# A linear-attention kernel: phi(K) of layer one's first two chunks summed on GpSimd instead of on TensorE

## The chip, the cores and the metric

The kernel runs on one core of one Trainium2 chip. The metric is device time in microseconds for one execution of the whole program. The core has five engines with a queue of instructions each: TensorE (PE, matrix products into PSUM), VectorE (DVE), ScalarE (ACT), GpSimd (POOL), and SyncE (SP, which here only starts DMAs). Each engine executes its queue in order; engines wait for one another through semaphores.

## The reference

The input x has 2048 tokens of 512 features in bfloat16. Two layers are applied, each one linear attention and one MLP, both with a layer norm before and a residual sum behind:

```python
phi = lambda t: where(t > 0, t + 1, exp(t)) + 1e-6
q, k, v = split(layernorm(x) @ wqkv)              # 32 heads of 16 features
pq, pk = phi(q), phi(k)
kv  = einsum("bhsd,bhse->bhde", pk, v)
z   = einsum("bhsd->bhd", pk)                     # sum of phi(K) over all tokens
num = einsum("bhqd,bhde->bhqe", pq, kv)
den = einsum("bhqd,bhd->bhq", pq, z) + 1e-6
x = x + (num / den) @ wo                          # attention half
x = x + gelu(layernorm(layernorm(x)) @ w1 + b1) @ w2 + b2   # MLP half
```

The MLP half norms twice, one norm upon the other. The change concerns `z`: the sum of phi(K) over the tokens, for the first layer.

## The kernel before

**Tiling.** The 2048 tokens are 16 tiles of 128, in four chunks of four tiles. Layer one (in the code layer 0) takes the chunks in the order `C0=(3, 0, 1, 2)`: tiles 12 to 15, 0 to 3, 4 to 7, 8 to 11. Its first stage is, for each tile: statistics of the norm (`stats`, `aggr` on VectorE; `veps`, `pow`, and `nmr` on GpSimd), the normed tile (`norm`, or `cen` and `ysc`), its transpose (`TA` by a DMA from SP's queue, or `PTA` on TensorE and `tcA`, a copy on ScalarE), the product for K (`K`), `exp` and `relu` on ScalarE and `min` and `phik` on VectorE, which leave phi(K) in a buffer of `pkb` (8 buffers), and `G`, four products that add yᵀ·phi(K) in PSUM. The Q products (`Q`) run between them, with `phiq`. At the end of the stage come `cpg` (G copied out), `KV`, `kvm` (a mask), `M`, `cpm`, and then `WO`, the output of the attention, `RA` (residual sum) and the MLP: `statsB` to `normB`, `TB`, `W1` with `gelu`, `W2`, `RB`. `b20` adds the bias b2.

**The sum z.** `attn_z` (line 898) has two ways, chosen by `ZC`, which says for each layer how many of the first chunks are summed the second way.

- For a chunk outside ZC, one operation `Z` is 16 matmuls (lines 937 to 946) of one column each: for each quarter of the features and each of the four tiles, 128x128 of phi(K) is loaded as weights and multiplied with a column of ones. A small VectorE operation (`zs`, line 948 or 951) copies the 128x4 result to `zs`, or adds it.
- For the chunks inside ZC the tiles are added one after another to a float32 accumulator `zacc` (`za`, line 914), on GpSimd unless a table says VectorE. Then VectorE makes a bfloat16 copy (`zhi`, the high half, line 920) and the rest (`zlo`, the low half, line 923), and one operation `ZH` sums both over the partitions with 8 matmuls of one column (lines 930 and 931). `zsh` (line 934) copies the result to `zs`.

```python
if n < cf["ZC"][L]:
    ...
    lambda e, second=second, k=k: e.tensor_tensor(
        zacc[:], pkb[:, zfirst[L].slot, :] if second else zacc[:], pkb[:, pks[k].slot, :], op=ALU.add),
```

Before, `ZC=(0, 3)`: layer one sums all four chunks with `Z0_3`, `Z0_0`, `Z0_1` and `Z0_2`; layer two adds its first three chunks, with seven of the eleven additions on GpSimd.

`zs` is needed at the end of the stage: `zb` (line 1022) makes the matrix with which `D` multiplies phi(Q) for the denominators (line 1085), and `dz` and `ZR` (lines 1027, 1030) make it once more in a row. `ln` and `rec` (lines 1087, 1089) turn D into 1/den on ScalarE, and `pr` multiplies it to phi(Q).

**Order.** The order of the instructions on each engine is written out by hand as lists (`ORDER`, one for each engine). A planner goes through these lists with a table of durations; it only gives out buffers and PSUM banks and then the semaphore waits. In the first stage PSUM leaves four of the eight banks to K, Q, transposes and the small products, since G holds the other four; a K or Q product waits until ScalarE and VectorE have read the bank that it takes. The W products and `WO` use banks 3 to 5.

**Queues.** SP's list holds the loads at the start, the transposes by DMA and the loads of b1 and b2. GpSimd's list holds, between its computations, the loads of `wv`, `wo`, and the halves of `w1` and `w2`; these wait until all transposes of the first stage have landed (`after=trs`, lines 1228 to 1237).

Of the kernel before, what the change touches and what calls it, by code (L numbers as in the profile page):

```python
# [282 lines left out]
def assign_waits(graph, order, sems, dma_sems):  # L283
# [10 lines left out]
    while len(done) < total:  # L294
        moved = False
        for e in ENGINES:
# [45 lines left out]
    C0=(3, 0, 1, 2), N_WARM=8, ZC=(0, 3), LQ='sp', N_HALF=1, N_K=4, N_Q=3, P_Z0=6.15, N_PB=1, N_PT=8, P_DEN=-50.43,  # L342
# [200 lines left out]
def build_kernel(nc, A_x, A_wqkv, A_wo, B_x, B_w1, B_b1, B_w2, B_b2, out, conf=None, report=False):  # L543
# [5 lines left out]
    with ExitStack() as es:  # L549
# [86 lines left out]

        C0 = cf["C0"]
        HC = C0[0]
        FIRST, LAST = 4 * HC, 4 * C0[-1] + 3
        x0 = [Tile(T4, f"x0_{c}") for c in range(NC)]  # L640
# [28 lines left out]
        load_chunk(cf["LQ"], C0[2], -96)  # L669
        load_chunk(cf["LQ"], C0[3], -95)  # L670

# [705 lines left out]
```

## Time and profile before

| what | value |
| --- | --- |
| time, median of 3 runs | 325.48 us (325.1 to 325.51) |
| profiled execution, own time | 325.25 us |
| its span (first to last instruction) | 323.5 us |
| PE busy | 318.4 us (98%) |
| VectorE, ScalarE, GpSimd busy | 216.5, 195.0, 134.8 us |
| granted TensorE clock | 1.000 |

Rows of a timeline give start and duration in us, engine, line, operation, output and input, and a count; in brackets is the idle time of the engine just before and what ended it. A row with x4 is four instructions in a run, and its duration runs from the first start to the last end. Matmuls overlap: in a dense run of 128x512 products one starts about 0.216 us behind the other (four in 0.865 us), though each is recorded with 0.379 us. VectorE's operations overlap a little too: the next begins some 0.08 us before the one ahead has ended. A row of a view by stretches gives, after the length of the stretch, the busy us of PE, PEld (weight loads), VectorE, ScalarE and GpSimd, each with a count, then the granted clock and the DMA's share.

### The profile page before, as it was taken

How to read it: one execution, taken by the hardware profiler on the slowest of the kernel's cores; microseconds unless marked ns; L12 is line 12 of the kernel's file. 1: busy time of each engine (PE TensorE's matmuls, PEld its weight loads, DVE VectorE, ACT ScalarE, POOL GpSimd, SP SyncE). 2: the span in 40 equal slices, each digit the busy share in tenths (PEclk: the TensorE clock that was granted, in tenths of full speed). 3: DMA queues.
4: the chain of work that ended last, by engine and by line, in shares of the span. 5: the costliest groups of instructions: out<-in, count | busy, mean ns of one | idle time of the engine just before them, and what ended most of it. 6: DMA issues, size and time to landing. Idle time of an engine off the chain costs nothing.

```text
span 323.5 us, 4765 instructions
## 1 busy us (share of the span) xinstructions
PE 318.4 (98%) x1698; PEld 159.9 (49%) x1729; DVE 216.5 (67%) x506; ACT 195.0 (60%) x336; POOL 134.8 (42%) x224
## 2 busy tenths in 40 slices
PE   8999999999999999999999999999999999999996
PEld 4444545675444444444444444458644444444443
DVE  4998769999985660213759999999999564000232
ACT  5999698773136129488964657789832644576000
POOL 4673268638703359000266645763541754000000
PEclk9999999999999999999999999999999999999999
DMA  7514558212320206310003200022133133000004
GB/s 239 181 38 91 151 148 290 72 34 56 75 49 9 41 16 99 66 32 2 0 0 68 49 16 2 17 55 47 36 63 82 32 51 81 16 0 2 32 28 152
DMA packets 47028, 20.39 MB, mean 63 GB/s; under 512 B 42076, under 2 KB 45532, under 8 KB 47004
## 3 DMA queue, kind: packets, MB, share of 16 engines
q1 hardware_dynamic: 45532, 15.06, 20.6%
q0 software_dynamic: 1056, 4.72, 4.5%
q10 hardware_dynamic: 416, 0.30, 0.3%
q8 instruction: 14, 0.23, 0.3%
q14 instruction: 10, 0.08, 0.1%
HBM read 8.00 MB, written 2.10 MB: 31 GB/s over the span
## 4 chain that ended last, share of the span: by engine, by line
PE 91%; DVE 7%; issue 1%
PE ps L1180 28%; PE ps L1141 26%; PE ps L860 8%; PE ps L1109 6%; PE ps L878 5%; PE ps L993 4%; PE ps L961 4%; PE ps L891 3%; DVE xsb L1114 2%; DVE stats L742 2%; PE ps L698 2%; DVE yb L782 1%; PE ps L1167 1%; DVE lr L1061 1%; PE ps L1085 1%; DVE rd L1064 1%
## 5 line engine op out<-in xcount | busy, mean ns | idle before, releaser
L1147 ACT ACTIVATE gT<-ps,b1c 128x512 bf16<-128x512 f32 (+1 forms) x140 | 77.0, 600 | 63.3 <-PE ps L1141 62.6
L1141 PE MATMUL ps<-t,w 128*128 128x512 bf16 (+1 forms) x556 | 101.2, 336 | 0.2
L1180 PE MATMUL ps<-w,gT 128*128 128x512 bf16 x424 | 97.6, 379 | 0.5
L1141 PEld LDWEIGHTS ps<-t,w 128*128 128x128 bf16 x560 | 54.7, 98 | 43.8 <-ACT t L815 0.3
L1180 PEld LDWEIGHTS ps<-w,gT 128*128 128x128 bf16 x434 | 42.5, 98 | 50.0
L757 POOL TENSOR_TENSOR rstd<-veps,neghalf 128x1 f32<-128x1 f32 x64 | 38.5, 612 | 5.2 <-DVE veps L755 3.1
L830 ACT ACTIVATE eb<-ps 128x512 bf16<-128x512 f32 x56 | 32.4, 600 | 13.1 <-PE ps L878 6.2
L1190 DVE TENSOR_TENSOR pkb<-ps,xsb 128x512 bf16<-128x512 f32 x15 | 10.1, 684 | 40.7 <-PE ps L1180 40.7
L742 DVE BATCH_NORM_STATS2 stats<-xsb 128x6 f32<-128x512 f32 x48 | 32.2, 677 | 0.3
L860 PE MATMUL ps<-wqkv,t 128*128 128x512 bf16 x125 | 31.1, 379 | 0.2
L1109 PE MATMUL ps<-gtb,t 128*128 128x512 bf16 x123 | 30.1, 379 | 0.3
L841 ACT ACTIVATE rb<-ps 128x512 bf16<-128x512 f32 x38 | 22.2, 601 | 8.9 <-PE ps L860 6.7
L747 POOL TENSOR_SCALAR veps<-mv 128x1 f32<-128x1 f32 x32 | 8.7, 272 | 44.6 <-DVE mv L744 42.2
L755 POOL TENSOR_SCALAR veps<-mv 128x1 f32<-128x1 f32 x28 | 7.2, 262 | 45.1 <-DVE mv L744 43.7
L777 ACT ACTIVATE yb<-xsb,nmr,rstd 128x512 bf16<-128x512 f32 x21 | 16.9, 810 | 11.6 <-POOL nmr L774 11.5
L782 DVE TENSOR_SCALAR yb<-xsb,mv,rstd 128x512 bf16<-128x512 f32 x27 | 14.8, 559 | 11.4 <-POOL rstd L757 11.2
L1186 DVE TENSOR_TENSOR xsb<-ps,xsb 128x512 f32<-128x512 f32 x16 | 10.9, 682 | 16.8 <-PE ps L1180 14.3
L843 DVE TENSOR_SCALAR eb<-eb 128x512 bf16<-128x512 bf16 x46 | 14.5, 329 | 7.8 <-ACT eb L830 7.6
L860 PEld LDWEIGHTS ps<-wqkv,t 128*128 128x128 bf16 x128 | 12.4, 98 | 14.6 <-ACT eb L830 0.3
L878 PE MATMUL ps<-wqkv,t 128*128 128x512 bf16 x76 | 19.4, 379 | 0.2
L1109 PEld LDWEIGHTS ps<-gtb,t 128*128 128x128 bf16 x128 | 12.4, 98 | 14.2 <-ACT gtb L974 0.5
L1126 POOL TENSOR_TENSOR xsb<-xsb,b2b 128x512 f32<-128x512 f32 x14 | 17.3, 1235 | 1.0 <-DVE yb L782 0.7
(103 smaller groups left out, 395.9 us busy)
## 6 DMA issues: line engine op xcount, KB each, us to landing
w<-in_B_w_dram POOLq DMA_DIRECT2D x4, 896.0 KB, 7.8
out_dram<-pkb SPq DMA_DIRECT2D x15, 128.0 KB, 2.0
t<-in_A_x_dram SPq DMA_DIRECT2D x3, 512.0 KB, 7.0
t<-yb SPq DMA_TRANSPOSE x56, 2.5
wqkv<-in_A_wqkv_dram SPq DMA_DIRECT2D x1, 512.0 KB, 5.4
wqkv<-in_A_wqkv_dram POOLq DMA_DIRECT2D x1, 512.0 KB, 4.4
wo<-in_A_wo_dram POOLq DMA_DIRECT2D x1, 512.0 KB, 5.1
t<-t SPq DMA_TRANSPOSE x20, 2.4
```

What stands on the lines that cost most here:

```text
L742: G.op("dve", lambda e: e.bn_stats(stats[:, s.slot, :], src()), 602, reads=src_keys, writes=[k + "s"], tiles=[s, *src_tiles], prio=prio, n ...
L757: G.op("pool", lambda e: e.tensor_tensor(rstd[:, s.slot:s.slot + 1], veps[:, s.slot:s.slot + 1], neghalf[:], op=ALU.pow), 530, reads=[k + ...
L782: G.op("dve", lambda e: e.tensor_scalar(yb[:, y.slot, :], src(), stats[:, s.slot, 2:3] if by_act else mv[:, s.slot, 0:1], rstd[:, s.slot:s ...
L830: G.op("act", lambda e: e.activation(eb[:, et.slot, :], bank(bt), ACT.Exp, scale=factor()), 569 if by else 483, reads=[src_key, *more], wr ...
L841: G.op("act", lambda e: e.activation(rb[:, rt.slot, :], bank(bt), ACT.Relu, scale=factor()), 569 if by else 478, reads=[src_key, *more], w ...
L860: ins = e.matmul(bank(b), lhsT=yTa(yT)[:, dt, k * P:(k + 1) * P], rhs=wqkv[:, dt, D:2 * D], start=(dt == 0), stop=(dt == DT - 1))
L878: ins = e.matmul(bank(b), lhsT=yTa(yT)[:, dt, k * P:(k + 1) * P], rhs=wqkv[:, dt, 0:D], start=(dt == 0), stop=(dt == DT - 1))
L1109: ins = e.matmul(bank(wb), lhsT=yTa(pq)[:, kt, k * P:(k + 1) * P], rhs=gtb[:, kt, :], start=(kt == 0), stop=(kt == DT - 1))
L1126: G.op("pool" if on_pool else "dve", lambda e: e.tensor_tensor(xsb[:, st, :], xsb[:, st, :], b2b[:], op=ALU.add), 1120 if on_pool else 600 ...
L1141: ins = e.matmul(bank(b, n), lhsT=w1[:, dt, ft * P:(ft + 1) * P], rhs=yTa(yT)[:, dt, k0 * P:k1 * P], start=(dt == 0), stop=(dt == DT - 1))
L1147: G.op("act", lambda e, ft=ft, b=b, k0=k0, k1=k1, n=n: e.activation(gT[:, g.slot, ft * 512 + k0 * P:ft * 512 + k1 * P], bank(b, n), ACT.Ge ...
L1180: ins = e.matmul(bank(b), lhsT=gT[:, g.slot, ft * 512 + k * P:ft * 512 + (k + 1) * P], rhs=w2[:, ft, :], start=(ft == 0), stop=(ft == FT - 1))
```

## The change

`ZC` goes from `(0, 3)` to `(2, 3)`. In layer one the chunks 3 and 0 are now summed the second way:

- `Z0_3` and `Z0_0` (16 matmuls each) and VectorE's `zs0_3` and `zs0_0` are gone.
- GpSimd has seven new additions of 128x512: `za0_13`, `za0_14`, `za0_15`, `za0_0`, `za0_1`, `za0_2`, `za0_3`.
- VectorE has `zhi0`, `zlo0` and `zsh0`; TensorE has `ZH0` with 8 matmuls. `Z0_1` and `Z0_2` stay, and are added to `zs`.

With it the lists of all five engines are new in the first stage, up to the first products of the MLP; from `W10_0_13_1` on TensorE's list is as before. No other operation is added, removed or given to another engine. The lines of the file behind the lists move down by one.

```diff
-    C0=(3, 0, 1, 2), N_WARM=8, ZC=(0, 3), LQ='sp', ...
+    C0=(3, 0, 1, 2), N_WARM=8, ZC=(2, 3), LQ='sp', ...
 pe:
-  "warm PTA0_12 idle0_0 PTA0_13 K0_12 idle0_1 K0_13 PTA0_14 Q0_3_0 Q0_3_2 PTA0_15 G0_12_0 K0_14 K0_15 "
-  "Q0_3_3 Q0_3_1 G0_13_0 PTA0_1 G0_14_0 K0_0 Z0_3 G0_15_0 K0_1 K0_3 K0_2 Q0_0_2 Q0_0_3 G0_0_0 G0_1_0 Q0_0_0 "
-  "K0_8 G0_2_0 G0_3_0 K0_5 Z0_0 K0_4 K0_6 K0_7 Q0_0_1 K0_10 K0_11 Q0_1_0 K0_9 Q0_1_3 Z0_1 G0_4_0 Z0_2 "
-  ...
-  "WO0_0_0 WO0_0_1 WO0_0_2 WO0_0_3 D0_1_3 WO0_1_0 WO0_3_0 WO0_2_0 Q0_2_3 WO0_5_0 WO0_4_0 WO0_6_0 PTB0_0 "
-  "WO0_7_0 W10_0_12_0 ..."
+  "warm PTA0_12 idle0_0 PTA0_13 K0_12 idle0_1 K0_13 PTA0_14 Q0_3_0 K0_14 PTA0_15 G0_12_0 Q0_3_3 K0_15 "
+  "PTA0_1 Q0_3_1 G0_13_0 K0_1 Q0_3_2 K0_0 G0_14_0 K0_3 G0_15_0 G0_0_0 Q0_0_3 Q0_0_2 K0_2 G0_1_0 K0_5 Q0_0_0 "
+  "G0_2_0 K0_4 K0_6 G0_3_0 K0_10 K0_8 G0_4_0 Q0_0_1 K0_7 G0_5_0 K0_11 K0_9 Q0_1_1 ZH0 Q0_1_3 Z0_1 Z0_2 "
+  ...
+  "WO0_0_0 WO0_0_1 WO0_0_2 WO0_0_3 D0_1_3 WO0_1_0 WO0_2_0 WO0_3_0 Q0_2_3 WO0_7_0 WO0_5_0 WO0_6_0 PTB0_0 "
+  "WO0_4_0 W10_0_4_0 ..."
 act:
-  "... expk0_13 reluq0_3_0 reluk0_13 tcA0_15 ..."
+  "... expk0_13 reluk0_13 expq0_3_0 tcA0_15 ..."
 dve:
-  "... mink0_14 yscA0_13 statsA0_10 normA0_1 yscA0_14 phik0_14 ..."
-  "... aggrA0_5 aggrA0_10 minq0_3_2 statsA0_8 zs0_3 phiq0_3_2 ... mink0_5 mink0_4 zs0_0 phik0_5 phik0_4 ..."
-  "... minq0_2_0 kvm0_2 kvm0_1 kvm0_0 kvm0_3 phiq0_2_0 cpm0_2 ..."
+  "... mink0_14 statsA0_8 statsA0_5 statsA0_7 normA0_2 ... mink0_0 aggrA0_7 phik0_0 statsA0_4 statsA0_6 ..."
+  "... statsA0_9 mink0_2 phik0_2 aggrA0_9 statsA0_11 aggrA0_11 phik0_3 ... phik0_7 zhi0 zlo0 mink0_11 phik0_11 mink0_9 zsh0 ..."
+  "... kvm0_0 kvm0_2 minq0_2_0 kvm0_1 kvm0_3 phiq0_2_0 cpm0_2 ..."
 pool:
-  "... vepsA0_2 powA0_2 vepsA0_5 powA0_5 nmrA0_5 vepsA0_8 powA0_8 vepsA0_10 ... powA0_11 nmrA0_9 phik0_6 w1_1 "
-  "phiq0_1_2 wv wo w2_1 phiq0_1_1 w1_0 pr0_0_2 pr0_1_0 pr0_1_1 w2_0 pr0_1_2 pr0_1_3 vepsB0_1 powB0_1 vepsB0_0 "
-  "powB0_0 b20_0 vepsB0_2 powB0_2 vepsB0_3 powB0_3 phiq0_2_3 pz0_2_1 ..."
+  "... vepsA0_2 powA0_2 za0_13 vepsA0_5 powA0_5 nmrA0_5 vepsA0_8 powA0_8 za0_14 ... powA0_10 nmrA0_6 za0_15 nmrA0_10 "
+  "powA0_7 za0_0 nmrA0_7 ... powA0_9 nmrA0_9 za0_1 za0_2 phik0_6 za0_3 wv w1_1 wo phiq0_1_2 w2_1 phiq0_1_1 pr0_1_0 "
+  "pr0_0_2 pr0_1_1 w1_0 w2_0 pr0_1_2 pr0_1_3 vepsB0_1 ... powB0_3 phiq0_2_3 b20_0 pz0_2_1 ..."
 sp:
-  "... TA0_11 TA0_9 b1 b2 Tb1 TB0_1 TB0_2 TB0_3 TP0_2_0 TB0_5 TB0_7 ..."
+  "... TA0_11 b1 TA0_9 Tb1 TB0_1 TB0_2 TB0_3 TP0_2_0 b2 TB0_5 TB0_7 ..."
```

More of the change, by code (lines that the diff above doesn't have):

```diff
@@ L341 @@
     LAND={'x0': 3220, 'x1': 4450, 'wk1': 5200, 'wk0': 6080, 'x2': 6750, 'wq': 8250, 'xc0': 9520, 'xc1': 10800, 'xc2': 12050},
-    C0=(3, 0, 1, 2), N_WARM=8, ZC=(0, 3), LQ='sp', N_HALF=1, N_K=4, N_Q=3, P_Z0=6.15, N_PB=1, N_PT=8, P_DEN=-50.43,
+    C0=(3, 0, 1, 2), N_WARM=8, ZC=(2, 3), LQ='sp', N_HALF=1, N_K=4, N_Q=3, P_Z0=6.15, N_PB=1, N_PT=8, P_DEN=-50.43,
     P_A2=-55.11, P_W1=38.59, P_W2=10.23, P_K=55.79, P_G=131.85, P_Q=170.13, STEP=3.86, A1_Q=12.91, A1_STEP=0.5, N_H=4,
```

107 rows, old and new, of the table ORDER are left out of this document.

## The prediction

> **What bounds the kernel now.** I read the page's first part, then busy time by stretches, then the waits of TensorE.
>
> ```profile
> span 323.5 us, 4765 instructions
> PE 318.4 (98%) x1698; PEld 159.9 (49%) x1729; DVE 216.5 (67%) x506; ACT 195.0 (60%) x336; POOL 134.8 (42%) x224
> ...
> PEclk9999999999999999999999999999999999999999
> ```
> ```profile
> 20.00:40.00 20.00, 19.89 (x134) 9.64 (x135) 16.25 (x50) 16.95 (x33) 8.87 (x20) 1.00 0.41 99
> 40.00:60.00 20.00, 19.89 (x105) 9.61 (x106) 17.02 (x37) 17.43 (x32) 14.35 (x17) 1.00 0.63 202
> 60.00:80.00 20.00, 19.84 (x148) 14.22 (x149) 19.96 (x49) 13.30 (x30) 11.76 (x18) 1.00 0.21 44
> 280.00:300.00 20.00, 19.95 (x92) 9.05 (x93) 0.91 (x2) 13.56 (x22) 0.00 (x0) 1.00 0.00 1
> ```
> ```profile
> PE ps L698 <- PEq L1362: 0.8, 1, 0.8
> ```
>
> TensorE is busy 19.84 to 19.95 of every 20 us, at the full clock, and its only listed wait is the start of the program. So it bounds the kernel from its first products to its last, and two things follow. Whatever leaves TensorE's queue is saved in full, and nothing beyond that can be saved. And every wait that a new order puts before a TensorE instruction is lost in full, because no gap stands behind it to take it up.
>
> **What TensorE loses.** Two groups of 16 one-column matmuls go, and one of 8 comes.
>
> ```profile
> 37.27 0.54 PE L942 MATMUL ps<-onesm,pkb 128*128 128x1 bf16 x16
> 37.67 1.02 PE L961 MATMUL ps<-pkb,yb 128*128 128x512 bf16 x4
> ```
>
> The group that stays in the same form, Z0_1, starts at 37.27 and the next operation at 37.67: 0.40 us for 16, 25 ns each. So 2 x 16 - 8 = 24 matmuls are 0.60 us. That is the gain, and also its ceiling: 0.18% of the time.
>
> The Trainium skill ("TensorE: Matmul & The Clock Gate", Back-to-back issue gap) gives about 81 ns for each pair of weight load and matmul in a sustained stream at 128 columns, because the weight load counts too; 24 such pairs would by that be worth an estimated 1.94 us. The two rows, with weight loads in them, show 25 ns, so I keep 0.60 and give the rule a small chance below.
>
> **What VectorE and GpSimd get.** The same operations stand in layer two.
>
> ```profile
> L914 POOL TENSOR_TENSOR zacc<-zacc,pkb x6: 1152/1248/1534, 166.0 to 187.1; 128x512 f32<-128x512 f32 x6
> L914 POOL TENSOR_TENSOR zacc<-pkb x1: 1157/1157/1157, 164.1 to 164.1; 128x512 f32<-128x512 bf16 x1
> L920 DVE TENSOR_SCALAR dz<-zacc x1: 414/414/414, 188.4 to 188.4; 128x512 bf16<-128x512 f32 x1
> L923 DVE TENSOR_TENSOR eb<-zacc,dz x1: 679/679/679, 188.9 to 188.9; 128x512 bf16<-128x512 f32 x1
> ```
> ```profile
> 10.00:18.00 8.00, 7.95 (x57) 4.02 (x57) 7.92 (x28) 8.00 (x15) 4.57 (x13) 1.00 0.38 103
> 18.00:26.00 8.00, 7.91 (x37) 3.56 (x37) 7.80 (x25) 7.56 (x15) 7.22 (x18) 1.00 0.18 38
> 26.00:34.00 8.00, 7.95 (x52) 3.81 (x51) 5.74 (x19) 7.84 (x15) 1.18 (x3) 1.00 0.48 97
> 34.00:42.00 8.00, 7.89 (x65) 4.07 (x66) 6.71 (x20) 5.55 (x11) 2.21 (x2) 1.00 0.42 134
> ```
>
> GpSimd gets 1.16 + 6 x 1.25 = 8.7 us. From 10 to 26 us it is busy 4.57 and 7.22 of 8, from 26 to 42 only 1.18 and 2.21. The list puts three additions in the first 16 us and four in the second, so there is room, though the norms' `pow` and `nmr` queue behind each addition and the transposes of later tiles wait for them. VectorE gets 0.41 + 0.68 us and one small copy, and loses two. It takes them after `phik0_7`, near 36 us, where 8.00 - 6.71 = 1.29 us of the stretch are idle. All of this is off TensorE's path as long as VectorE's phi and norm arrive in time, so in itself I cost it at nothing. The cover is VectorE's idle time: 0.28 us from 10 to 26, but 2.26 + 1.29 = 3.55 us from 26 to 42.
>
> **The additions hold VectorE.** This is the cost that the trace of before shows only in layer two.
>
> ```profile
> 176.91 1.15 POOL L914 TENSOR_TENSOR zacc<-zacc,pkb 128x512 f32<-128x512 f32 x1
> ```
> ```profile
> 177.74 0.48 DVE L843 TENSOR_SCALAR eb<-eb 128x512 bf16<-128x512 bf16 x1 [0.69 <-ACT eb L830]
> ```
> ```profile
> L843 DVE TENSOR_SCALAR eb<-eb x46: 230/288/877, 8.5 to 237.2; 128x512 bf16<-128x512 bf16 x46
> ```
>
> An addition runs from 176.91 to 178.06. The `min` that VectorE starts at 177.74 takes 0.48 instead of the median 0.29: it got going near the end of the addition. So one addition holds a fast VectorE operation for anything from 0 (VectorE is in statistics or in a read of PSUM) to its whole 1.15 us. The new list runs `za0_13` beside three statistics and `za0_14` beside `phik0_0`, which reads PSUM, and two statistics: near 0. The other five lie beside `min`, `phik` and `norm`. I take half a length, about 0.6 us, for each: the order on both engines is fixed, but where in an addition the fast operation falls is not. That is 5 x 0.6 = 3.0 us, less than the 3.55 us of idle time. What remains for TensorE are places where a bank or a phi(K) comes late: `phik0_2` before G0_2, right behind `za0_15`, where TensorE is due as it ends, and `phik0_4`, which frees the bank of K0_8. I take 0.20 us for both. The ends: 0, and 5 x 1.15 - 3.55 = 2.20 us.
>
> The Trainium skill says the same more sharply ("SBUF — State Buffer", Who interferes with whom): the port pair of VectorE and GpSimd is an exclusive lock, and whoever is second fully blocks. The 0.48 agrees with a block until shortly before the end; the rule speaks against this change and stands behind the second rival.
>
> **A new wait at the head.** Before, G0_12 and K0_14 lay between the transpose PTA0_15 and K0_15, the first product that needs tile 15 (`tcA0_15`). Now K0_14 runs ahead of PTA0_15, and Q0_3_3, which needs tile 15, follows G0_12 at once.
>
> ```profile
> 8.58 0.60 ACT L815 ACTIVATE t<-ps 128x512 bf16<-128x512 bf16 x1
> ...
> 10.77 0.63 ACT L815 ACTIVATE t<-ps 128x512 bf16<-128x512 bf16 x1
> ```
> ```profile
> 9.22 0.11 PEld L878 LDWEIGHTS ps<-wqkv,t 128*128 128x128 bf16 x2 [0.33 <-ACT t L815]
> ```
> ```profile
> 11.19 0.38 PE L860 MATMUL ps<-wqkv,t 128*128 128x512 bf16 x1
> ```
>
> The copy at 8.58 (`tcA0_14`) let a weight load go at 9.22, 0.64 us later. ScalarE has the same number and kinds of operations ahead of `tcA0_15` as before, so that still starts at 10.77 and releases at 11.41; TensorE is free for it at 11.19 (where K0_14 started). Cost 0.22 us, bounds 0.15 to 0.30 by what ScalarE's operations scatter. In the old order K0_14 covered it.
>
> **The end of the stage.** `minq0_2_0` ran in a wait for TensorE; now it stands between the four masks `kvm`.
>
> ```profile
> 49.79 0.28 DVE L834 TENSOR_SCALAR eb<-eb 128x512 bf16<-128x512 bf16 x1
> 50.39 0.88 DVE L1035 TENSOR_TENSOR kvb<-ps,bdmask 128x128 bf16<-128x128 f32 x4 [0.32 <-PE ps L1016]
> ...
> 57.88 0.54 DVE L782 TENSOR_SCALAR yb<-xsb,mv,rstd 128x512 bf16<-128x512 f32 x1
> ```
> ```profile
> 58.45 6.67 SPq L792 DMA_TRANSPOSE t<-yb  x3
> ```
> ```profile
> 61.00 8.48 PE L1141 MATMUL ps<-t,w 128*128 128x256 bf16 x76
> ```
>
> From 50.39 VectorE runs without a gap to `normB0_1` at 57.88; its transpose leaves at 58.45, and the first W1 product, at 61.00, needs it. So VectorE is nearly as late as TensorE here, and 0.2 us more before it is 0 to 0.2 us for TensorE: I take 0.10.
>
> **Steps moved past queues.** GpSimd now starts `w1_0` after `pr0_1_1` instead of ahead of the three `pr`, and SP starts `b2` behind TP0_2_0.
>
> ```profile
> 50.04 2.40 POOL L1093 TENSOR_TENSOR t<-t,lr 128x512 bf16<-128x512 bf16 x2 [0.45 <-ACT lr L1089]
> ```
> ```profile
> w<-in_B_w_dram POOLq DMA_DIRECT2D x4, 896.0 KB, 7.8
> ```
> ```profile
> 66.28 1.19 SPq L1077 DMA_TRANSPOSE t<-t  x1
> ```
> ```profile
> b2b<-in_B_b_dram SPq DMA_DIRECT2D x1, 128.0 KB, 3.1
> ```
> ```profile
> t<-yb SPq DMA_TRANSPOSE x56, 2.5
> ```
> ```profile
> 69.44 1.15 POOL L1061 TENSOR_TENSOR lr<-t,zrow 128x512 f32<-128x512 bf16 x1 [1.75 <-DVE t L847]
> ```
> ```profile
> 72.24 0.65 DVE L1064 TENSOR_REDUCE rd<-lr 128x32 f32<-128x512 f32 x1
> ```
> ```profile
> 79.35 1.26 SPq L792 DMA_TRANSPOSE t<-yb  x1
> ```
> ```profile
> 82.75 1.46 PE L1141 MATMUL ps<-t,w 128*128 128x256 bf16 x8
> ```
>
> `w1_0` leaves at about 52.4 and lands 7.8 us later, at 60.2, against a need at 61.00: hidden by 0.8. `wv` and `wo` leave earlier than before and are no danger. `b2` leaves at 66.28 + 1.19 = 67.5 and lands at about 70.6. `b20_0` waits for it, and behind it on GpSimd `pz0_2_1` (69.44 before) goes to about 71.8 and ends at 73.0. VectorE's `red0_2_1` at 72.24 needs it and comes about 0.8 us late, with all that is behind, down to `normB0_4`, whose transpose left at 79.35. A transpose lands 2.5 us later, so near 82.7 instead of 81.9. The first product of the next chunk is the fifth of the row at 82.75; four of the smaller ones ahead of it take 4 x 8.48 / 76 = 0.45, so it is due at 83.2. Hidden by 0.5: nothing. `b1` now goes ahead of TA0_9, which is wanted by the last K product of the stage, and `b20_0` itself is wanted only by the residual sum behind W2: nothing. A buffer of phi(K) is now held until its addition is done; the last one, tile 3's, is taken by `phik0_9`, the last phi(K) in VectorE's list: nothing.
>
> **The sum.** -0.60 + 0.22 + 0.20 + 0.10 = -0.08 us. Made against the profiled execution's 325.25 us it is 325.2; the median of the runs stands 0.23 higher, at 325.48, so 325.4. About 0.2% (0.65 us) is what a measurement of this kernel can tell from no change.
>
> **The rivals.**
>
> *All of the gain stays* (chance 0.13): ScalarE reaches `tcA0_15` earlier and the additions fall beside statistics. 325.48 - 0.60 = 324.9. For it: TensorE had no wait in the old order, which was as tight. Against it: the head's wait hangs on ScalarE, which is busy 8.00 of 8.
>
> *The additions push VectorE behind TensorE* (0.24): slower. Place: from `za0_15` to `za0_3`. The price is 5w - 3.55 us for an average hold w. With the 0.28 of gain that the head and the end leave (0.60 - 0.32), the kernel is slower by over 0.65 once 5w - 3.55 exceeds 0.93, so from w = 0.90 on; at w = 1.15 it is 2.20 - 0.28 = 1.9 us slower, 327.4. I would expect some 326.4 in this case. For it: VectorE's lists are mostly fast operations there. Against it: 0.19 us was the hold in the row above.
>
> *A moved load comes late* (0.15): `w1_0` at W1's start, or `b2` through `red0_2_1` and TB0_4. For it: four steps hang on `b2` in a stretch where VectorE is busy 19.96 of 20. Against it: both are hidden by the medians. It decides when `w1_0` takes over 61.00 - 52.4 = 8.6 us, or when TB0_4 lands after 83.2; 1.2 us more than reckoned on the second path costs 1.2 - 0.5 = 0.7, so about 326.1.
>
> *Weight loads count too* (0.02): the one-column matmuls cost 81 ns where they stand between big ones; then 325.48 - 1.94 + 0.52 = 324.1.
>
> **How the numbers follow.** My forecast, the gain taken back by small waits, has 0.46, with its own range of 325.0 to 325.9. Faster by over 0.65 us can come from the last rival and from a part of the first, whose 0.60 lies just short of it and whose runs scatter by 0.41 us (325.1 to 325.51): 0.02 + 0.05 = 0.07. Slower: 0.22 of the second rival, 0.10 of the third, 0.05 of the forecast's tail: 0.37. Same is the rest, 0.56. The range goes from 324.8, just under the whole gain, to 326.9, inside the second rival, of which the dearer third stays out.
>
> **What would show it.** In the new profile Z's line should have 48 matmuls instead of 80 and line 931 twice four; TensorE should show a wait of about 0.2 us near 11.2 on ScalarE's copy. Between 24 and 36 us `min` and `phik` on VectorE should be recorded up to a microsecond longer beside an addition. If TensorE's rows between 26 and 38 us run on without a gap, the second rival is wrong; if W1's first product starts at 60.5 or before, the end of the stage costs nothing; if `b20_0` starts by 68 or VectorE has no wait near 72, the move of `b2` was free. The prediction is wrong if a wait of a microsecond or more shows on TensorE anywhere, or if its waits add up to less than 0.2 us.

## The result, and the profile after

Over nine executions of each kernel the change took the time from 325.17 to 326.96 us (medians): a ratio of 1.0051, with a 95% interval of 1.004 to 1.0061. So the kernel became slower by about 1.7 us, 0.5%. The forecast was 325.4, with a range up to 326.9; the time lies just above the range, on the side that had a chance of 0.37. The profiled execution of the changed kernel took 327.28 us, with a span of 325.5, against 325.25 and 323.5 before. Behind the lists every line number is one higher than before.

The page's first part, the waits of TensorE, and the stretches:

```profile
span 325.5 us, 4758 instructions
PE 320.0 (98%) x1705; PEld 157.8 (48%) x1705; DVE 220.8 (68%) x507; ACT 195.1 (60%) x336; POOL 144.1 (44%) x231
```
```profile
PE ps L1142 <- issue: 0.9, 1, 0.9
PE ps L699 <- PEq L1363: 0.8, 1, 0.8
PE ps L962 <- DVE pkb L837: 0.5, 1, 0.5
PE ps L1142 <- DMA t<-yb: 0.3, 1, 0.3
```
```profile
26.00:34.00 8.00, 7.54 (x36) 3.18 (x34) 7.66 (x19) 7.30 (x14) 7.00 (x13) 1.00 0.36 74
60.00:80.00 20.00, 19.05 (x145) 13.81 (x144) 18.63 (x45) 12.66 (x29) 11.30 (x17) 1.00 0.26 46
```

Where one wait stood, at the start of the program, there are now four. Two of the new ones show in the stretches: from 26 to 34 us TensorE is busy 7.54 us instead of 7.95, and from 60 to 80 us 19.05 instead of 19.84. (The counts of matmuls can't be compared: some records are missing in each trace.) The two places, in the timeline:

```profile
25.45 1.03 PE L892 MATMUL ps<-t,wqkv 128*128 128x512 bf16 x4
26.94 1.04 PE L962 MATMUL ps<-pkb,yb 128*128 128x512 bf16 x4 [0.46 <-DVE pkb L837]
```
```profile
60.47 1.04 PE L1110 MATMUL ps<-gtb,t 128*128 128x512 bf16 x4
62.45 8.46 PE L1142 MATMUL ps<-t,w 128*128 128x256 bf16 x76 [0.95 <-issue]
```

The first is G0_2. The four products ahead of it take 0.865 us, so it was due at 26.32 and is 0.62 late. The second is the first W1 product: it starts 1.98 us behind the start of the last WO group, where it was 61.00 - 60.13 = 0.87 before.

To see all of the difference I cut the span at six instructions of TensorE: the first Q product (Q0_3_0), the first M product (the end of the first stage), the last WO group, the first W1 product, the WO products of the last chunk, and the matmul ZR of layer two. Each number is the difference of the starts of two rows; the runs below the first three are those of the next section.

```
kernel       start..Q0_3_0  ..M    ..last WO  ..W1   ..WO, last chunk  ..ZR    ..end   span
before           8.36      42.69    9.08      0.87      29.52         105.06   127.9   323.5
after            8.15      43.18    9.14      1.98      29.49         105.21   128.4   325.5
s1 (after)       8.56      42.91    9.13      2.24      29.49         105.20   128.0   325.5
e2               8.37      42.69    9.08      1.81      29.49         105.06   127.9   324.4
s2               8.63      43.18    9.14      0.87      29.64         105.12   128.3   324.9
s4               8.49      43.24    9.14      0.87      29.54         105.29   127.9   324.5
s3               8.78      42.70    9.08      0.88      29.55         105.06   128.0   324.0
e3               8.43      42.60    9.12      1.37      29.49         105.15   128.0   324.2
r12              8.81      42.61    9.13      0.88      29.55         105.21   127.9   324.1
r9               8.17      43.79    9.13      2.08      29.49         105.06   127.9   325.6
```

The start scatters between 8.15 and 8.81 from execution to execution in kernels of either kind; the wait of 0.3 at 246 us (the column before the span) also comes and goes. The rest is the change's: +0.2 to +0.5 in the first stage, although 0.60 us of matmuls left it; +1.1 and +1.4 at the first W1 product; and +0.15 between the last chunk's WO and ZR, over 100 us behind the last instruction that was moved.

### The profile page after: what moved, and what is told of

Same layout as the page of the kernel before. It is cut to its first block, busy times and chain, and to the rows that moved or that the text cites. A ratio compares the mean times of both kernels' runs of the same rounds, so it can differ in the third digit from the quotient of the medians.

```text
span 325.5 us, 4758 instructions
## 1 busy us (share of the span) xinstructions
PE 320.0 (98%) x1705; PEld 157.8 (48%) x1705; DVE 220.8 (68%) x507; ACT 195.1 (60%) x336; POOL 144.1 (44%) x231
## 4 chain that ended last, share of the span: by engine, by line
PE 87%; DVE 7%; ACT 2%; DMA 2%; issue 1%; POOL 1%; ACTq 0%
PE ps L1142 29%; PE ps L1181 25%; PE ps L1110 8%; PE ps L861 7%; PE ps L994 4%; PE ps L879 4%; PE ps L962 3%; PE ps L892 2%; DVE stats L743 1%; DMA t<-yb 1%; ACT eb L831 1%; PE ps L1168 1%; DVE xsb L1115 1%; PE ps L1086 1%; DMA t<-in_A_x_dram 1%
## 5 line engine op out<-in xcount | busy, mean ns | idle before, releaser
L758 POOL TENSOR_TENSOR rstd<-veps,neghalf 128x1 f32<-128x1 f32 x64 | 39.3, 626 | 4.9 <-DVE veps L756 3.0
L861 PE MATMUL ps<-wqkv,t 128*128 128x512 bf16 x128 | 32.0, 379 | 0.2
L1110 PE MATMUL ps<-gtb,t 128*128 128x512 bf16 x128 | 30.9, 379 | 0.0
L844 DVE TENSOR_SCALAR eb<-eb 128x512 bf16<-128x512 bf16 x46 | 15.3, 344 | 7.8 <-ACT eb L831 7.7
L879 PE MATMUL ps<-wqkv,t 128*128 128x512 bf16 x80 | 20.4, 379 | 0.1
```

The source lines that it names most:

```text
L758: G.op("pool", lambda e: e.tensor_tensor(rstd[:, s.slot:s.slot + 1], veps[:, s.slot:s.slot + 1], neghalf[:], op=ALU.pow), 530, reads=[k + ...
L861: ins = e.matmul(bank(b), lhsT=yTa(yT)[:, dt, k * P:(k + 1) * P], rhs=wqkv[:, dt, D:2 * D], start=(dt == 0), stop=(dt == DT - 1))
L879: ins = e.matmul(bank(b), lhsT=yTa(yT)[:, dt, k * P:(k + 1) * P], rhs=wqkv[:, dt, 0:D], start=(dt == 0), stop=(dt == DT - 1))
L1110: ins = e.matmul(bank(wb), lhsT=yTa(pq)[:, kt, k * P:(k + 1) * P], rhs=gtb[:, kt, :], start=(kt == 0), stop=(kt == DT - 1))
```

## The experiments

The theory after the first look was that the first W1 product waits because w1_0, which now leaves GpSimd right ahead of w2_0, holds up the transpose TB0_1 that W1 needs; and that the rest is VectorE, held by the additions. The rivals were that the late VectorE behind the moved b2 and b20_0 is what costs, and that the new order costs by itself. Where an expectation names a theory by a letter, A is the load of w1, B the additions as the whole loss, C the late b2, D the load of w1 and the late b2 side by side, of which TensorE pays the larger, and E that the late b2 costs nothing.

### The load of w1

**e2**: the kernel before, with only w1_0 moved.

```diff
 pool (before):
-  "... w2_1 phiq0_1_1 w1_0 pr0_0_2 pr0_1_0 pr0_1_1 w2_0 ..."
+  "... w2_1 phiq0_1_1 pr0_0_2 pr0_1_0 pr0_1_1 w1_0 w2_0 ..."
```

> The kernel before, without any addition, with the one step moved the other way: w1_0 behind pr0_1_1, directly ahead of w2_0 (52.4 instead of 47.66). Theory A: TB0_1 lands 3.5 us or more after its issue at 58.45, the first W1 product goes from 61.00 to about 62.1, and the kernel takes 326.3 us instead of 325.2. Theories B and C: 325.2, within 0.2, since neither the additions nor b2 are in it.

Measured: 1.0035 (1.0024 to 1.0046), about 1.1 us. The table has all of it in one column, 1.81 instead of 0.87. In e2's timeline:

```profile
61.95 8.46 PE L1141 MATMUL ps<-t,w 128*128 128x256 bf16 x76 [0.78 <-issue]
```

Why, is seen in what the DMA engines do around TB0_1. After, both halves leave in one run (the row below); before, w1_0 left at 47.66 and w2_0 at 52.38, behind three `pr`.

```profile
52.80 1.73 POOL L683 DMA_DIRECT2D w<-in_B_w_dram  x2
```

The first half, w1_0, is in time: it lands 4.9 us after its issue, at 57.7. But w2_0, right behind it, lands at 61.8, where before it landed at 60.3. TB0_1 leaves SP's queue at 58.45 before, at 58.79 after and at 58.46 in e2, where the stretches of one microsecond from 58 on read, before and after (the last two columns are the DMA engines' share and GB/s):

```profile
58.00:59.00 1.00, 1.00 (x6) 0.45 (x5) 1.00 (x3) 1.00 (x4) 0.75 (x2) 1.00 0.07 29
```
```profile
58.00:59.00 1.00, 1.00 (x6) 0.49 (x5) 1.00 (x3) 1.00 (x3) 0.83 (x3) 1.00 1.01 393
```

And the time from issue to landing of that one transpose, before, after, and in e2:

```profile
DMA to landing us min/median/max: 2.4/2.4/2.4
```
```profile
DMA to landing us min/median/max: 3.6/3.6/3.6
```
```profile
DMA to landing us min/median/max: 3.4/3.4/3.4
```

With w2_0 still in flight the transpose takes 1.0 to 1.2 us longer. Full DMA engines at its issue are not enough for that: in e5, a run shown further down, TB0_1 leaves at 59.30, from 59 to 60 the share is 1.05 at 365 GB/s, and it still lands after 2.4 us. Its own data, 544 small packets, start to move only about 1.2 us after the issue, when most of the load is through. These are the DMA views of 2 us from there, after (from 60.0), in e5 (from 60.4) and in e2 (from 59.2): packets, MB, and the time that they took as a share of 16 engines. Queue q1 carries the transpose, q0 the load, q8 instructions.

```profile
q1 hardware_dynamic: 535, 0.13, 71.2%
q0 software_dynamic: 12, 0.04, 5.3%
```
```profile
q1 hardware_dynamic: 544, 0.13, 32.8%
q0 software_dynamic: 4, 0.00, 0.7%
```
```profile
q1 hardware_dynamic: 544, 0.13, 69.7%
q0 software_dynamic: 20, 0.02, 4.1%
q8 instruction: 1, 0.02, 3.4%
```

Undisturbed, the packets of the transpose take 32 to 33% (before, e4, e5). After, 12 packets of the load are left when they begin, and come one or two at a time until 61.3; 44 packets of the transpose follow only from 61.2 on. In e2 the load is through when they begin, at 59.6, but one packet with instructions, which started at 59.2, takes 1.1 us of an engine. The same holds in the other slow traces: s1 and e3 have packets of the load left, r9 has an instruction packet. So TB0_1 seems to be late because a single DMA engine is late. That it is one engine is not shown outright, since the views don't name the engine of a packet; it is read from the packets that come singly.

**s1**: the changed kernel once more, unaltered, for the scatter of this wait.

> The changed kernel as it is, once more, as the base line for the other runs of this group and for a second trace of W1's start. 1.6 us above the kernel before. If the wait at W1's start is the rule with w1_0 in its new place, it is there again, 0.8 us or more; if it comes and goes, it may be 0 to 1.0.

Measured: 1.0042 (1.0028 to 1.0055). The wait is there again, 1.20 us, the landing 3.8 us. Over all runs with w1_0 directly ahead of w2_0 (after, s1, e2, r9, e3, e4, e5) TB0_1 landed after 3.6, 3.8, 3.4, 3.7, 3.0, 2.4 and 2.4 us: the wait comes in five of seven traces. In the eleven traces with w1_0 earlier (before, e1, e6, e7, e8, r10, r11, r12, s2, s3, s4) it was 2.4 or 2.5 each time, without a wait. In e4 and e5 the loads are as close together, but the load's last packets of 4 KB are through when the transpose's begin, at 60.2 and 60.5; w2_0 lands 7.0 us after its issue there, against 7.6 to 8.5 in the five slow traces. Why the end of the load varies so from execution to execution stays open.

**e1**: w1_0 ahead of the `pr`, about where it was before. **s2**: w1_0 much earlier, right behind `wo`.

```diff
 pool (after), e1:
-  "... phiq0_1_1 pr0_1_0 pr0_0_2 pr0_1_1 w1_0 w2_0 ..."
+  "... phiq0_1_1 w1_0 pr0_1_0 pr0_0_2 pr0_1_1 w2_0 ..."
 pool (after), s2:
-  "... wo phiq0_1_2 ... pr0_1_1 w1_0 w2_0 ..."
+  "... wo w1_0 phiq0_1_2 ... pr0_1_1 w2_0 ..."
```

> The changed kernel with one step moved: GpSimd starts w1_0 right behind phiq0_1_1 again, ahead of pr0_1_0, pr0_0_2 and pr0_1_1 (about 48.6 us instead of 52.80). Theory A (the late load: w1_0 and w2_0 leave together at 52.80, still occupy the DMA engines when the transpose TB0_1 leaves at 58.79, and W1's first product waits for it): TB0_1 lands 2.4 to 2.6 us after its issue instead of 3.6, the first W1 product starts near 61.4 instead of 62.45, and the kernel takes about 325.9 us, 1.1 less than the 326.96 of the changed kernel. Theory B (the additions hold VectorE, and the whole loss comes from there): 327.0, within 0.2. Theory C (b2 comes late for b20_0 and VectorE's red0_2_1): 327.0, within 0.2.

> The changed kernel with w1_0 right behind wo on GpSimd (near 38.7 us, where GpSimd has nothing to do, so that no pr is pushed back), buffers and PSUM banks as in the changed kernel, b2 and b20_0 left late. Theory A alone (the late w1_0 costs W1's start about a microsecond, b2's move costs TensorE nothing in these banks): 0.9 us below the changed kernel, 0.7 to 0.8 above the kernel before. Theory D (TensorE pays the larger of the two, so b2's part is still paid): no gain against the changed kernel.

Measured: e1 1.0052 (1.004 to 1.0064), no gain at all; s2 1.0032 (1.0019 to 1.0045). In both the wait at W1 is gone, TB0_1 lands after 2.5 us. In e1 part of what was gained there is lost again elsewhere, 0.42 us between M and the last WO (9.56 against 9.14): issuing the load keeps GpSimd for 0.76 us, the products of den behind it move back by that much, and now one of them lies beside VectorE's `minq0_2_0`, between the masks for M, which takes 0.72 us instead of 0.28:

```profile
51.57 0.72 DVE L835 TENSOR_SCALAR eb<-eb 128x512 bf16<-128x512 bf16 x1
```

Behind `wo` nothing of VectorE's is in the way, and the table has 0.87 for s2 in that column, as before the change. The profiled span of s2 is 0.6 us shorter than that of after and s1: less than the column's 1.1 and 1.4. Against after, s2 loses 0.15 behind W1 and began 0.48 later; against s1 it also has the wait at 246 us and a longer stage. Between the ratios lie 0.3 to 0.6 us; if the wait doesn't come in every execution, the ratios hold only a part of it.

### The load of b2 and its addition

**e4**, **e5**: in the changed kernel, b2 back to its old place, and in e5 b20_0 too. **e8**: in the kernel before, both moved to their new places.

```diff
 sp (after), e4 and e5:
-  "... b1 TA0_9 Tb1 TB0_1 TB0_2 TB0_3 TP0_2_0 b2 TB0_5 ..."
+  "... b1 TA0_9 b2 Tb1 TB0_1 TB0_2 TB0_3 TP0_2_0 TB0_5 ..."
 pool (after), e5 also:
-  "... powB0_0 vepsB0_2 ... phiq0_2_3 b20_0 pz0_2_1 ..."
+  "... powB0_0 b20_0 vepsB0_2 ... phiq0_2_3 pz0_2_1 ..."
 sp and pool (before), e8: the same two moves the other way
```

> The changed kernel with one step of SP moved: b2 ahead of Tb1 (near 34 us) instead of behind TP0_2_0 (67.98). Theories A and B: 327.0 us, within 0.2, b20_0 starting some 2 us earlier and no TensorE row before 80 us moving. Theory C: red0_2_1 and what is behind it on VectorE come earlier, and the kernel gains 0.4 us or more: 326.5 or less.

> Theory D: two late steps lie side by side, each good for about a microsecond, and TensorE pays the larger: W1's start through the transposes behind w1_0 and w2_0 (1.0 in the profile of the changed kernel, none in that of the last experiment), and near 76 us the bank that RB0_1 on VectorE frees, behind b2, b20_0 and pz0_2_1. Here b2 goes ahead of Tb1 and b20_0 behind powB0_0 as in the kernel before, and w1_0 stays late. D: RB0_1 comes about 1.3 us earlier, no TensorE wait near 76, but W1's start may still wait, by 0 to 1.0 us from one execution to the next: 0.4 to 1.4 us above the kernel before, and a wide scatter. Theory E (the move of b2 and b20_0 does nothing, since VectorE is late for other reasons, the additions' lock): 1.6 us above the kernel before, as the changed kernel.

> The kernel before, without any addition, with b2 behind TP0_2_0 on SP and b20_0 behind phiq0_2_3 on GpSimd as in the changed kernel. Theory D: pz0_2_1 and with it red0_2_1 on VectorE come about 1.3 us late, RB0_1 too, and TensorE waits near 76 us for its bank: 0.8 to 1.3 us above the kernel before. Theory E and the prediction's own reckoning (hidden by 0.5): within 0.2 of the kernel before.

Measured: e4 1.0054 (1.0042 to 1.0066), e5 1.0031 (1.0019 to 1.0042), e8 1.0037 (1.0025 to 1.005). By e8 the move of b2 would cost 1.2 us. But e4 and e8 each have a wait of about a microsecond on PSUM that neither kernel has, in e8:

```profile
90.72 1.04 PE L1141 MATMUL ps<-t,w 128*128 128x512 bf16 x4 [0.96 <-DVE xsb L1186]
```

The planner hands out the PSUM banks by going through the lists, and with b20_0 elsewhere it gave this W1 product the bank of another residual sum, one that is read later. So both runs have two changes in one, and show nothing of the load. In e5 the banks are those of the changed kernel; but that profile was one of the two without a wait at W1, so it too has two causes.

**s3**: as e8, with the two steps moved behind the planner's work, so that every bank stays as before. **s4**: e5 with w1_0 as in s2.

```diff
 s3, behind the planner:
     order = sch.run()
+    for q, n, to in (("pool", "b20_0", "pz0_2_1"), ("sp", "b2", "TB0_5")):
+        o = order[q].pop([o.name for o in order[q]].index(n))
+        order[q].insert([o.name for o in order[q]].index(to), o)
```

> The kernel before with b2 behind TP0_2_0 and b20_0 ahead of pz0_2_1, moved after the planner has given out buffers and banks, so that these are all as in the kernel before (in the earlier run with this move the planner gave W10_1_0_0 the bank that RB0_2 frees, not RB0_3). Theory A alone, and the prediction's reckoning: VectorE is about 1.2 us late from red0_2_1 on, but TensorE does not wait for it: within 0.2 of the kernel before. Theory D: 0.8 us or more above it, as in the earlier run.

> The changed kernel with w1_0 right behind wo and b2 and b20_0 at their old places, banks as in the changed kernel. Theory A alone: the same as with w1_0 behind wo only, 0.7 to 0.8 us above the kernel before. Theory D: the only one of this group that gains against the changed kernel, by 0.9.

Measured: s3 0.9999 (0.999 to 1.0008); s4 1.0024 (1.0015 to 1.0033). In s3 the steps are late: GpSimd stands still for 3.09 us until b2 has landed, and `red0_2_1` on VectorE starts at 73.90 instead of 72.24, of which 0.44 is the later start of this execution (W1 at 61.44 against 61.00). TensorE has no wait for it (29.55 from W1 to the last chunk, against 29.52):

```profile
71.15 1.15 POOL L1126 TENSOR_TENSOR xsb<-xsb,b2b 128x512 f32<-128x512 f32 x1 [3.09 <-DMA b2b<-in_B_b_dram]
```
```profile
73.90 0.69 DVE L1064 TENSOR_REDUCE rd<-lr 128x32 f32<-128x512 f32 x1 [0.22 <-POOL lr L1061]
```

So the late b2 costs nothing; that rival falls, and what e8 seemed to show was the bank. s4 is the fastest of the variants with whole additions, and is still 0.8 us slower than the kernel before.

### The additions

**e3**: the additions of layer one, from the second on, on 32 of the 512 columns, so that z leaves those tiles out in the other columns. **r12**: the same, with b2 and b20_0 as in e5 and w1_0 as in s2.

```diff
-    lambda e, second=second, k=k: e.tensor_tensor(
-        zacc[:], pkb[:, zfirst[L].slot, :] if second else zacc[:], pkb[:, pks[k].slot, :], op=ALU.add),
+    lambda e, second=second, k=k, w=D if second or L else 32: e.tensor_tensor(
+        zacc[:, 0:w], pkb[:, zfirst[L].slot, 0:w] if second else zacc[:, 0:w], pkb[:, pks[k].slot, 0:w], op=ALU.add),
```

> The changed kernel with its additions on GpSimd cut to 32 of the 512 columns from the second addition of layer one on (the sum z of the first two chunks leaves these tiles out in the other columns), all lists as they are: each of the six takes about 0.1 to 0.2 us instead of 1.15. Theory A: only the waits of the stage of K and G go, above all the 0.46 us ahead of G0_2, so about 326.3 us, and W1's first product still waits about a microsecond. Theory B: the loss goes as a whole, 325.2 us or, with the 0.60 us of TensorE's work that is saved, down to 324.6. Theory C: 327.0.

> Everything undone but the new order of the first stage and TensorE's smaller work: b2 and b20_0 at their old places, w1_0 right behind wo, and the additions of layer one from the second on cut to 32 of 512 columns (the sum z leaves these tiles out in the other columns). If the loss is the sum that the traces give so far (the moved queue steps, 0.58 us of lock ahead of G0_2, 0.2 us near 186 us), the stage of K and G takes about 42.6 us from Q0_3_0 to M, no TensorE wait is listed besides the start, and the kernel takes 0.0 to 0.3 us more than the kernel before. If something is not accounted for: 0.6 us or more above it.

Measured: e3 1.0019 (1.0009 to 1.0029), r12 1.0006 (0.9997 to 1.0016). In the changed kernel the `min` ahead of G0_2's phi(K) runs beside `za0_15` (VectorE, then GpSimd, then VectorE again):

```profile
25.36 0.79 DVE L835 TENSOR_SCALAR eb<-eb 128x512 bf16<-128x512 bf16 x1
26.19 0.69 DVE L837 SCALAR_TENSOR_TENSOR pkb<-ps,eb 128x512 bf16<-128x512 f32 x1
```
```profile
24.85 1.15 POOL L915 TENSOR_TENSOR zacc<-zacc,pkb 128x512 f32<-128x512 f32 x1
```

With the narrow additions of r12 it takes 0.28, and G0_2 starts with no wait in brackets, 0.96 behind the start of the operation ahead (26.11), so 0.10 late instead of 0.62:

```profile
26.01 0.28 DVE L835 TENSOR_SCALAR eb<-eb 128x512 bf16<-128x512 bf16 x1
```
```profile
24.93 0.25 POOL L915 TENSOR_TENSOR zacc<-zacc,pkb 128x32 f32<-128x32 f32 x1
```
```profile
27.07 1.04 PE L962 MATMUL ps<-pkb,yb 128*128 128x512 bf16 x4
```

The stage falls from 43.18 to 42.60 and 42.61 us: the additions' hold on VectorE costs TensorE 0.58 us there, some 0.53 of it at this place. (In s1, where G0_2 is 0.54 late, the stage takes 42.91, and the hold is worth 0.3.) But without any hold the stage is only 0.09 us shorter than before, though 0.60 us of matmuls are gone. So the new lists cost about 0.5 us by themselves. In r12 all of it shows as gaps between dense runs: 0.27 ahead of Q0_3_3, 0.13 ahead of K0_0, the 0.10 at G0_2 and 0.03 ahead of K0_3. The first is the wait for `tcA0_15` that the prediction names for the head. PTA0_15 starts at 10.54; its four products take 0.22 and the four of G0_12 0.865, so Q0_3_3 was due at 11.62:

```profile
10.54 0.39 PE L806 MATMUL ps<-idp,yb 128*128 128x128 bf16 x4
11.89 1.04 PE L879 MATMUL ps<-wqkv,t 128*128 128x512 bf16 x4
```
```profile
11.89 0.55 PEld L879 LDWEIGHTS ps<-wqkv,t 128*128 128x128 bf16 x4 [0.59 <-ACT t L816]
```

**r11**: the hold moved instead of removed. Loads as in r12, additions whole, and `za0_15` one norm step later, with the banks kept.

```diff
 r11, behind the planner:
     order = sch.run()
+    names = [o.name for o in order["pool"]]
+    za = order["pool"].pop(names.index("za0_15"))
+    order["pool"].insert([o.name for o in order["pool"]].index("za0_0"), za)
+    nm = order["pool"].pop([o.name for o in order["pool"]].index("nmrA0_7"))
+    order["pool"].insert([o.name for o in order["pool"]].index("za0_15"), nm)
```

> The changed kernel with b2 and b20_0 at their old places, w1_0 right behind wo on GpSimd (near 38.7 us, where GpSimd has nothing to do), and za0_15 behind nmrA0_7, all buffers and PSUM banks as in the changed kernel. If G0_2's wait is the lock of za0_15 alone, TensorE has no wait there and the stage of K and G is 0.5 us shorter; W1's start has no wait. 0.3 to 0.6 us above the kernel before, from the new order of the stage and the 0.2 near 186 us. If the additions only shift their hold to another place that TensorE waits for, as the kernel with only b2 and b20_0 moved: 1.0 above the kernel before.

Measured: 1.0034 (1.0022 to 1.0047), no better. G0_2 has no wait in brackets any more, and a K product waits instead:

```profile
31.71 1.04 PE L861 MATMUL ps<-wqkv,t 128*128 128x512 bf16 x4 [0.50 <-DVE pkb L837]
```
```profile
27.62 1.45 DVE L844 TENSOR_SCALAR eb<-eb 128x512 bf16<-128x512 bf16 x2
```
```profile
26.14 2.57 POOL L915 TENSOR_TENSOR zacc<-zacc,pkb 128x512 f32<-128x512 f32 x2
```

Two `min` take 1.45 us instead of 0.48 beside two additions, and K0_8 waits for its bank behind `phik0_4`.

**r10**: the additions in the lists of before, without the new search.

> The seven additions, zhi0, zlo0, ZH0 and zsh0 put into the lists of the kernel before, which stay in all else: za0_13 behind powA0_2, za0_14 behind powA0_8, za0_15 and za0_0 behind nmrA0_6, za0_1 and za0_2 behind nmrA0_9, za0_3 behind phik0_6; zhi0 and zlo0 ahead of mink0_9, ZH0 ahead of Q0_1_3. No queue step of b2, b20_0 or w1_0 is moved. If the loss lies in the moved queue steps and in the new order of the first stage alone, the kernel gains: 0.60 saved less 0.2 near 186 us, 325.1 or 0.3 below the kernel before. If the additions hold VectorE in any order for about as much as VectorE has idle, 0 to 0.6 above it. Theory B of the first runs in its strong form: 1 us or more above it.

Measured: 1.026 (1.0243 to 1.0277), 8.2 us. TensorE waits 2.7 us for phi(K) and 2.1 us for the low half:

```profile
PE ps L961 <- DVE pkb L847: 2.7, 3, 1.2
PE ps L930 <- DVE eb L923: 2.1, 1, 2.1
```

Here too the banks came out otherwise, so the 8.2 us are not the additions' alone. That the additions need an order made for them is plain from the waits; what this one costs is the 0.5 us of e3 and r12.

**e6** and **e7**: three old places at once (e5 with e1's w1_0), and in e7 also `za0_15` later, in the lists.

> The same, and w1_0 ahead of the three pr as in the kernel before, so that all three moved queue steps are undone while the additions and all other orders stay. Theory D: neither W1's start nor the bank near 76 us is waited for; what is left are the 0.6 us ahead of G0_2 and 0.3 to 0.4 us in the masks (minq0_2_0 held by a pr on GpSimd) against the 0.60 that is saved: 0.2 to 0.6 us above the kernel before, 1.0 or more below the changed one. Theory E: still 1.0 us or more above the kernel before.

> The same, with za0_15 moved behind nmrA0_7 on GpSimd, directly ahead of za0_0, so that it starts about a microsecond later, when mink0_2 is through. If the 0.46 us ahead of G0_2 are the lock of za0_15 on mink0_2 and nothing else, G0_2 comes 0.4 to 0.6 us earlier and the kernel takes 0.5 less than the last one: about the time of the kernel before, within 0.3. If another operation of VectorE then delays it as much, no change against the last one.

Measured: e6 1.0035 (1.0023 to 1.0048), e7 1.0158 (1.0144 to 1.0172). e6 has e1's held `min` between the masks and so gains nothing over e5. e7 has other banks again, and waits of 1.0 and 0.8 us for them at the WO products; it says nothing of its edit, and r11 took its place.

### The 0.15 us far behind

Between the last chunk's WO and ZR no order was changed. In the trace of the changed kernel a transpose that lands near 186 us is slow, beside a packet of the instruction queue (the DMA view from 179 to 186 us, after):

```profile
q8 instruction: 1, 0.02, 0.8%
t<-yb SPq DMA_TRANSPOSE x3, 3.3
```

The products behind it wait for their weights:

```profile
186.18 1.41 PEld L861 LDWEIGHTS ps<-wqkv,t 128*128 128x128 bf16 x8 [0.46 <-DMA t<-yb]
```

Before, the same view has no such packet from 179 to 186 us and a median of 2.4; its packet stands in the view from 175 to 178, where no transpose was issued:

```profile
q8 instruction: 1, 0.02, 1.8%
```

TensorE has 48 instructions fewer in the new kernel (24 matmuls and their weight loads), and the packets that carry instructions come later. **r9** puts 24 pairs back, in the first stage: ZH0 four times.

```diff
 r9 (e5, and):
-    for kt in range(DT):
+    for kt in list(range(DT)) * (1 if L else 4):
```

> The changed kernel with b2 and b20_0 at their old places, and ZH0 done four times over: 24 matmuls of one column and their weight loads more, so that TensorE has as many instructions as in the kernel before. Theory F (the 0.2 us that the changed kernel and all its variants lose near 186 us come from the fetch of TensorE's instructions: with 48 instructions fewer its packets fall at 182 to 183 us, on the transposes of layer two, and not at 176): the packets fall where they fell before, the transpose issued near 181 us lands after 2.5 us instead of 4.2, and TensorE goes from WO of the last chunk (90.5) to layer two's ZR (195.6) in 105.06 us instead of 105.2 to 105.3. ZH0 itself costs 24 x 25 ns = 0.60 us more at 38 us. Together 0.4 us above the kernel with only b2 and b20_0 moved, 1.4 above the kernel before. Rival: the fetch is chance or of another engine, the transposes still land after 4.2 us, 1.6 above the kernel before.

Measured: 1.0066 (1.0053 to 1.0079). From the last chunk's WO to ZR it takes 105.06 us, as before, and the landings of that stretch, in the changed kernel and in r9, are:

```profile
DMA to landing us min/median/max: 2.4/3.3/4.2
```
```profile
DMA to landing us min/median/max: 2.4/2.5/2.5
```

So the count of instructions shifts which transpose meets a packet, and that costs the 0.15 us. The other traces agree (r10 apart, which is some 10 us behind by then): in the five with the packet at 176 to 178 us (before, e2, e8, s3, r9) the way from WO to ZR takes 105.06 or 105.07 us, in the twelve with it at 181 us or later 105.12 to 105.29. The stage is 0.60 us longer than in e5 (43.79 against 43.19): 24 pairs, 25 ns each. The total is more than these two make, because the wait at W1 came back in r9 (1.04 us).

## Why the prediction was wrong

By its own steps:

- *What bounds the kernel*: right. Every wait that the new order put before TensorE was lost in full, and the sum of the table's columns is the whole difference.
- *0.60 us less on TensorE*: right. ZH0's eight matmuls start at 38.20 and the next product at 38.42, and r9's 24 more pairs took 0.60, 25 ns each. The rival by which weight loads count too falls; the Trainium skill's 81 ns ("TensorE: Matmul & The Clock Gate", Back-to-back issue gap) is a figure for 128 columns, and doesn't carry over to these pairs of one column.
- *The head, 0.22*: right, in place and nearly in size. Q0_3_3 starts 0.26 or 0.27 late in eleven of the thirteen traces with the new list on TensorE (r12 above). In the profiled execution of the changed kernel it is 0.03 and in r9 0.13: after, G0_12 starts at 10.11, so Q0_3_3 was due at 10.98 and starts at 11.00, since ScalarE reached `tcA0_15` 0.44 us behind the start of the transpose PTA0_15 (9.89) instead of 0.68 as in r12:

```profile
10.33 0.61 ACT L816 ACTIVATE t<-ps 128x512 bf16<-128x512 bf16 x1
```
```profile
10.11 1.03 PE L962 MATMUL ps<-pkb,yb 128*128 128x512 bf16 x4
11.00 1.04 PE L879 MATMUL ps<-wqkv,t 128*128 128x512 bf16 x4
```

- *The additions hold VectorE*: right in kind and in place. From 8 to 50 us the fast operations on VectorE grew, in the view by groups, before and after:

```profile
L843 DVE TENSOR_SCALAR eb<-eb 128x512 bf16<-128x512 bf16 x19 | 5.2, 286 | 0.8 <-ACT eb L830 0.6
L847 DVE TENSOR_TENSOR t<-eb,rb 128x512 bf16<-128x512 bf16 x7 | 2.9, 415 | 0.3 <-ACT rb L841 0.3
```
```profile
L844 DVE TENSOR_SCALAR eb<-eb 128x512 bf16<-128x512 bf16 x19 | 6.1, 329 | 0.9 <-ACT eb L831 0.8
L848 DVE TENSOR_TENSOR t<-eb,rb 128x512 bf16<-128x512 bf16 x7 | 3.6, 523 | 0.3 <-ACT rb L842 0.2
```

  With the other two groups of `min` and `phik` and the norm it is about 2.7 us by the means, against 3.0 in the prediction. G0_2, named there as the first place, is where it is paid. The term was mis-sized: 0.20 was taken, some 0.53 at G0_2 and 0.58 in the stage measured. The idle time of VectorE that was to cover it lies elsewhere in the stage; at G0_2 there was none. As the other half of the term, K0_8's bank, nothing was paid after; it was in r11. The longest of these operations, 1.15 and 1.16 us, stand beside two additions of 1.19 us each:

```profile
31.10 1.15 DVE L844 TENSOR_SCALAR eb<-eb 128x512 bf16<-128x512 bf16 x1
32.45 1.16 DVE L848 TENSOR_TENSOR t<-eb,rb 128x512 bf16<-128x512 bf16 x1 [0.20 <-ACT rb L842]
```
```profile
30.95 2.38 POOL L915 TENSOR_TENSOR zacc<-zacc,pkb 128x512 f32<-128x512 f32 x2
```

  That agrees with the full block of the Trainium skill ("SBUF — State Buffer", Who interferes with whom).
- *The end of the stage, 0.10*: nothing. M to WO takes 1.73 us in both kernels, and with w1_0 early (s2, s4) W1 starts 0.87 behind the last WO, as before.
- *Steps moved past queues, nothing*: **this is the step that failed.** For b2 it was right, link by link (s3). For w1_0 it compared the load's landing with the need for it, and the load was indeed in time, at 57.7. It didn't ask what the step does to the load behind it, w2_0, and to the transpose that the first W1 product waits for, which was in the prediction's own rows (58.45): with w1_0 directly ahead, packets of w2_0 are left when that transpose's packets come, and the transpose lands 3.6 and 3.8 us after its issue instead of 2.4. This is 1.1 and 1.4 us of TensorE in the two traces of the changed kernel. The Trainium skill ("DMA: Bandwidth & Descriptors", Queues, rings and completion order) has each DMA engine go round between the queues that hold work for it, a packet at a time. No run here shows that going round, since the views don't tell the engines apart. The third rival had the place, W1's start, but another mechanism, a late load.
- *Not in the prediction at all*: the other half of what the new order of the first stage costs by itself, about 0.25 us (0.13 ahead of K0_0, 0.10 at G0_2 without any hold, 0.03 ahead of K0_3), and the 0.15 us of the instruction packets.

The sum from the runs: -0.60 for the matmuls, +0.5 for the order, half of it the head's wait, +0.58 for the hold, +0 to 1.4 for the transpose at W1 (1.1 and 1.4 in two traces), +0.15 for the packets: 1.7 to 2.0 where the wait occurs and 0.6 where it doesn't, against 2.0 between the profiled spans and 1.4 (s1) and 1.7 by the ratios. Open is why the load ends so differently from execution to execution, which decides whether TB0_1 is slow, and with it how much of the 1.1 to 1.4 us a median run pays.

## What to carry to other kernels

When a load is moved, check it not only against its own consumer but against every transfer that is in flight beside it and has no slack; here a load that arrived in time cost a microsecond through a transpose. Where an engine has no gap, an order that is free of waits is itself worth something: of the 0.60 us that left TensorE, 0.5 went into the order that made room for the additions, and a hold that was moved from one place came back at another. And one execution is thin evidence for a small wait: the head's 0.27 us is missing from the very trace in which one would look for it first. Where a planner gives out buffers from the order, keep the buffers fixed when a single step is tried; four of the sixteen runs (e4, e7, e8, r10) measured other banks instead of their edit.

## What the runs showed of the hardware

- A 128x512 transpose by DMA landed 2.4 to 2.5 us after its issue. Where packets of a load were left when its own packets began, or an instruction packet of 1.1 us ran beside them, it took 3.0 to 3.8 us (five traces). A share of 1.05 at 365 GB/s that ended just before did not slow it (e5).
- Instructions come over the same DMA engines. 48 instructions fewer on TensorE moved a packet of that queue onto a stretch with transposes, where one landed after 4.2 us instead of 2.5, and TensorE lost 0.15 us, over 100 us behind the last moved instruction (five traces against twelve).
- One-column matmuls with 128x128 weights each started 25 to 26 ns apart, also in r9's run of 32 (38.23 to 39.05).
- A GpSimd addition on 32 columns took 0.25 us and left a `min` beside it at 0.28 us; on 512 columns 1.15 us, with a `min` of up to 1.15 us.
